# A recurrent attention kernel on one core: the ring for streamed weights goes from six places to five, and 17 instead of 18 weight units are streamed

## The chip, the core and the metric

The kernel runs on one core of one Trainium2 chip. The metric is the device time of one execution in microseconds (us). Before the change it is 1967.8 us, the median of three runs from 1961.2 to 1968.58.

The engines that matter here are TensorE (PE; PEld loads its weights), VectorE (DVE), ScalarE (ACT), and SyncE (SP), which issues nearly all transfers from memory. Each engine works through its own instructions in the order of the program and waits for the others at semaphores. Transfers run on 16 DMA engines that all issuers share.

## The reference, cut to what matters

Two branches work on the normalised input, and both are added to `x`. Branch A is attention with a recurrent memory; branch B is a dense layer pair with gelu.

```python
# S = 2048 rows, Dm = 1024, H = 32 heads of 128, M = 8 memory rows, 32 rows in a segment
mem = mem0
for s in range(64):                                  # one segment after the other
    h = concatenate([mem, xs], axis=1)               # 8 + 32 rows
    q = einsum('btd,dhe->bhte', h, Wq)               # 1024 x 4096 each
    k = einsum('btd,dhe->bhte', h, Wk)
    v = einsum('btd,dhe->bhte', h, Wv)
    p = softmax(where(mask, q k^T * scale, -1e9))
    o = einsum('bhte,hed->btd', p v, Wo)             # 4096 x 1024
    mem = o[:, :M, :]                                # the next segment needs it
    outs.append(o[:, M:, :])
# ...
return x + A(xn, mem0) + B(xn)                       # B: gelu(xn w1 + b1) w2 + b2
```

Each segment needs the 8 memory rows that the segment before it puts out, so the 64 segments can't be run side by side, and each of them needs all four weight matrices. Those have 4 x 8 MB in bf16, which is more than the on-chip memory holds beside everything else.

## The kernel before

Branch B runs first (some 420 us). Then come the 64 segments. The attention weights are cut into 64 units of 128 x 2048 bf16 (0.5 MB). A segment uses them in a fixed order: six half passes of 8 units (K and Q for the first half of the heads, K and Q for the second, V first half, V second half), and then 16 units of O. I write K0 to K7 for the units of a half pass, and O0 to O15 for those of O.

```python
NUNIT = 64
STREAMED = 18
LEAD = 6
LATER = 3
STREAM_BUFS = 6

def pass_order():
    order = []
    for w, u in (("K", 0), ("Q", 0), ("K", 1), ("Q", 1), ("V", 0), ("V", 1)):
        for i in range(KT):                          # KT = 8
            order.append((w, i, u))
    for ch in range(2):
        for j in range(4):
            for u in range(2):
                order.append(("O", ch * 4 + j, u))
    return order

ORDER = pass_order()
PLACED = "S....S.." "..S....S" "...S...S" "...S...S" "....S..." ".S.S..S." ".S..S..S" "..S..S.S"
IS_STREAMED = {unit: PLACED[n] == "S" for n, unit in enumerate(ORDER)}
RESIDENT = [unit for unit in ORDER if not IS_STREAMED[unit]]

IN_PSUM = [unit for unit in ORDER if IS_STREAMED[unit]][3]
HALF = [unit for unit in ORDER[48:] if IS_STREAMED[unit]][3]
```

46 units are loaded once and stay on the chip (resident). The 18 marked with S pass in each segment through a ring of six places. Two of the 18 are not read from memory after the first segment: IN_PSUM lies in two banks of PSUM (`kept`), and HALF lies half in a bank and half in a home of its own. VectorE copies them from the banks into a ring place, in pieces of 128 x 1024.

```python
RING = [f"xn{k}" for k in range(4)] + [f"w1_{k}" for k in range(16)]
RES_PLACES = list(low) + ["xt0", "xt1"] + RING[STREAM_BUFS:]   # places for residents
RING = RING[:STREAM_BUFS]
# ...
streams = [unit for _ in range(NSEG) for unit in ORDER if IS_STREAMED[unit]]
late_by = [
    LATER if unit == HALF or (unit == IN_PSUM and n >= STREAMED) else 0 for n, unit in enumerate(streams)
]
starts = deque(sorted(range(len(streams)), key=lambda n: (n + late_by[n], late_by[n])))

def start_stream(slot):
    n = starts.popleft()
    unit, t = streams[n], slab(slot)
    if unit in kept_in:
        for c0, bank in kept_in[unit]:
            nc.vector.tensor_copy(out=t[:, c0:c0 + 1024], in_=bank)        # L228
    elif unit in copies:
        nc.sync.dma_start(out=t[:, :], in_=copies[unit])                   # L230
    # ...

def unit_done(unit):
    if IS_STREAMED[unit]:
        start_stream(slot_of.pop(used - 1))          # the place just read takes the next start
        # ...
```

So the n-th start goes out when the streamed unit of six places earlier has been used. The starts of the two kept units stand three places later in the order than their use does (LATER).

A half pass multiplies the 32 rows of the segment with eight units; at some segments a second set of 32 rows (`hL`, the left rows, the last eight of each of four segments) is multiplied with the same units.

```python
def product(w, i, t, lhs, acc, seq):
    for j in range(4):                               # four column groups of TensorE, 128 x 512 each
        nc.tensor.matmul(o, lhsT=lhs[:, i, :], rhs=m, ..., tile_position=(0, 32 * j))      # L690

def half_pass(w, u, left, at):
    # ...
    for i in range(KT):
        t = unit_tile((w, i, u))
        product(w, i, t, hT, ps, range(KT))
        if left and i not in ahead:
            product(w, i, t, hL, psL, order)
        unit_done((w, i, u))
        for fn in at.get(i, ()):
            fn()                                     # scores, sums, values of the half before
    return ps, psL

for s in range(NSEG):
    g, i4 = divmod(s, GRP)                           # GRP = 4: four kinds of segment
    # left rows: K first half at i4 == 3, K second at 0, Q first at 1, Q second at 2,
    #            V first at 0, V second at 3, and twice the columns in O at i4 == 1
    psK, psKL = half_pass("K", 0, left_k[0], {})
    turn_k(psK, 0)                                   # ACT cast L734, then DVE transpose L748: kT
    psQ, psQL = half_pass("Q", 0, left_q[0], {})
    q_left(0)
    turn_q(psQ)                                      # ACT cast, DVE transpose: q_home (in b_oL)
    psK1, psK1L = half_pass("K", 1, left_k[1], {})
    # ... transposes; scores(0) after Q unit 0, sums(0) after Q unit 7
    psQ1, psQ1L = half_pass("Q", 1, left_q[1], at)
    # ...
    psV, psVL = half_pass("V", 0, left_v[0], {})
    at = {0: [scores(1)], 2: [values(0, 0)], 4: [values(0, 1)], 6: [sums(1)]}   # cut
    psV1, psV1L = half_pass("V", 1, left_v[1], at)
    at = {4: [values(1, 0)], 6: [values(1, 1)]}      # cut
    for n, unit in enumerate(O_UNITS):
        t = unit_tile(unit)
        o_product(unit, t, psX)                      # L870
        unit_done(unit)
        for fn in at.get(n, ()):
            fn()
    # psX -> o_sb (ACT L954); up to LEAD = 6 products of the next segment's left rows are made here
    put_mem(o_sb, nxt["hT"], ...)                    # L262 on TensorE, then DVE L266 into hr
```

Of the kernel before, what the change touches and what calls it, by code (L numbers as in the profile page):

```python
# [17 lines left out]
S = 2048  # L18
# [23 lines left out]


NUNIT = 64
STREAMED = 18
LOW = 3
SCRATCH = 512
SMALL = 3584
LEAD = 6
LATER = 3  # L50
STREAM_BUFS = 6


def pass_order():
# [11 lines that stand above are left out]


ORDER = pass_order()
PLACED = "S....S.." "..S....S" "...S...S" "...S...S" "....S..." ".S.S..S." ".S..S..S" "..S..S.S"
IS_STREAMED = {unit: PLACED[n] == "S" for n, unit in enumerate(ORDER)}  # L70
assert PLACED.count("S") == STREAMED
RESIDENT = [unit for unit in ORDER if not IS_STREAMED[unit]]

IN_PSUM = [unit for unit in ORDER if IS_STREAMED[unit]][3]
HALF = [unit for unit in ORDER[48:] if IS_STREAMED[unit]][3]
assert len(RESIDENT) == NUNIT - STREAMED


@with_exitstack
def kernel(  # L80
# [102 lines left out]
    RING = [f"xn{k}" for k in range(4)] + [f"w1_{k}" for k in range(16)]  # L183
    RES_PLACES = list(low) + ["xt0", "xt1"] + RING[STREAM_BUFS:]
    RING = RING[:STREAM_BUFS]
    for k in range(7):
# [19 lines left out]
    def fetch_resident(*places):  # L206
# [7 lines left out]
    late_by = [  # L214
        LATER if unit == HALF or (unit == IN_PSUM and n >= STREAMED) else 0 for n, unit in enumerate(streams)
    ]
# [828 lines left out]
```

The softmax here doesn't subtract the row's maximum and nothing guards it: scores larger than these inputs give would overflow.

## Time and profile before

| | before |
|---|---|
| median of 3 runs | 1967.8 us |
| span of the profiled execution | 1969.5 us |
| PE busy | 1774.1 us (90%) |
| DVE busy | 886.2 us (45%) |
| ACT busy | 599.5 us (30%) |
| DMA moved | 627.06 MB, mean 318 GB/s over the span |
| share of queue q1 (SyncE's transfers) | 82.3% of 16 engines over the span |

The share of an engine over the whole span mixes two stages. In branch B (to about 420 us) TensorE works without a pause and the DMA moves little: 123 GB/s in the first 330 us, with 40% of the DMA engines' time. In the 64 segments the DMA moves 368 GB/s. The change touches the second stage, so windows of that stage are what to look at.

A wait row of the profile names who waited, at which line, for whom, and then the total us, how many times, and the longest. "Issue" as releaser means that the engine stood while nothing that the profile shows released it. A row of the timeline has its start, its duration, engine, line, operation and tiles, and in brackets the idle time of the engine before it with its releaser. Buffer numbers are left out: `u` is any resident or ring place, `Wc_O` any copy of a streamed O unit in memory, `kept` the PSUM banks.

### The profile page before, as it was taken

To read this page: it belongs to the slowest core of one execution; us is meant where nothing else is said; L and a number is where in the kernel's file an instruction comes from. 1 tells how busy PE (TensorE), PEld (TensorE's weight loads), DVE (VectorE), ACT (ScalarE), POOL (GpSimd) and SP (SyncE) were. 2 spreads that over 40 slices of the span, in tenths; PEclk is the share of its full clock that TensorE was granted. 3 is DMA by queue.
4 is the path that set the end of the run, shared out by engine and by line. 5 is a ranking of instruction groups with operands and counts; after the bars stand their busy time and mean duration, and the time that the engine had idled before them with its cause. 6 is when DMAs were issued, how large, how long until landed. Compare 5 with 4: busy or idle time off the path is not lost.

```text
span 1969.5 us, 77311 instructions
## 1 busy us (share of the span) xinstructions
PE 1774.1 (90%) x34307; PEld 980.5 (50%) x34307; DVE 886.2 (45%) x2280; ACT 599.5 (30%) x1355; POOL 276.2 (14%) x538
## 2 busy tenths in 40 slices
PE   7999999989888989888989889889888889899887
PEld 3444444445545544455555545455446445545544
DVE  6656565414444444344444444344444444444433
ACT  6343434312223323222222222223222222222222
POOL 0000000002421112121112111111111111111111
PEclk9999999999999999999999999999999999999999
DMA  9821212789999999999999999999999999999998
GB/s 331 252 55 43 55 43 54 283 308 341 381 381 375 388 366 365 354 356 364 378 358 385 370 363 367 363 358 379 359 356 353 380 338 370 383 369 366 367 369 308
DMA packets 219883, 627.06 MB, mean 318 GB/s; under 512 B 47211, under 2 KB 65307, under 8 KB 219548
## 3 DMA queue, kind: packets, MB, share of 16 engines
q1 hardware_dynamic: 199132, 601.96, 82.3%
q0 software_dynamic: 16320, 17.52, 2.7%
q8 instruction: 268, 4.39, 0.9%
q10 hardware_dynamic: 4096, 2.64, 0.4%
q14 instruction: 67, 0.55, 0.1%
HBM read 607.77 MB, written 30.47 MB: 324 GB/s over the span
## 4 chain that ended last, share of the span: by engine, by line
PE 69%; DMA 16%; issue 7%; DVE 4%; ACT 2%; POOL 1%; ACTq 0%; DVEq 0%; POOLq 0%; SPq 0%
PE acc L690 29%; PE acc L870 15%; PE ps L483 10%; DMA u<-Wc_O 8%; PE ps L532 7%; DMA out_dram<-res 4%; PE ps L567 2%; DMA u<-Wc_V 2%; PE mixed L844 2%; DMA u<-Wc_Q 1%; POOL out_dram L1007 1%; PE acc L844 1%; DVE b_oL L748 1%; PE mixed L794 1%; DVE d_oL L899 1%
## 5 line engine op out<-in xcount | busy, mean ns | idle before, releaser
L690 PE MATMUL acc<-u,hr 128*32 128x512 bf16 x11520 | 789.6, 382 | 28.0 <-issue 15.3
L690 PEld LDWEIGHTS <-hr 128*32 128x32 bf16 x12288 | 354.6, 97 | 291.1 <-issue 62.1
L690 PE MATMUL acc<-u,hrL 128*32 128x512 bf16 x2880 | 265.2, 393 | 25.6 <-issue 13.8
L870 PE MATMUL acc<-u,d_oL 128*32 128x256 bf16 (+1 forms) x3552 | 192.6, 297 | 25.5 <-DMA u<-Wc_O 13.9
L483 PE MATMUL ps<-u 128*128 128x512 bf16 x896 | 195.9, 382 | 2.6 <-ACT u L367 2.6
L870 PEld LDWEIGHTS <-b_oL 128*32 128x32 bf16 (+1 forms) x3552 | 117.1, 104 | 81.9 <-issue 48.8
L870 PE MATMUL acc<-u,b_oL 128*32 128x256 bf16 (+1 forms) x1554 | 119.5, 305 | 30.8 <-issue 29.1
L532 PE MATMUL ps<-u 128*128 128x512 bf16 x672 | 147.0, 379 | 0.0
L228 DVE COPY u<-kept 128x1024 bf16<-128x1024 bf16 x190 | 125.0, 686 | 42.4 <-PE acc L690 19.7
L483 PEld LDWEIGHTS <-u 128*128 128x128 bf16 x896 | 88.1, 98 | 109.2 <-issue 4.0
L870 PEld LDWEIGHTS <-d_oL 128*32 128x32 bf16 (+1 forms) x3552 | 103.4, 100 | 69.2 <-issue 44.2
L690 PEld LDWEIGHTS <-hrL 128*32 128x32 bf16 x3072 | 92.9, 98 | 89.8 <-issue 47.8
L266 DVE CAST hr<-mixed 128x64 bf16<-128x64 f32 x63 | 14.1, 224 | 259.1 <-PE mixed L262 249.5
L870 PE MATMUL acc<-W_O,b_oL 128*32 128x256 bf16 (+1 forms) x1776 | 115.5, 307 | 12.9 <-issue 12.9
L748 DVE STREAM_TRANSPOSE b_oL<-b_oL 128x512 bf16<-128x512 bf16 x128 | 90.6, 708 | 61.1 <-ACT b_oL L734 61.1
L844 PEld LDWEIGHTS <-v 32*128 32x128 bf16 x2048 | 64.3, 91 | 101.3 <-issue 70.8
L924 POOL DMA_DIRECT2D res<-hr_d x59 | 33.2, 562 | 537.2 <-PE mixed L825 297.4
L734 ACT CAST kT<-acc 128x512 bf16<-128x512 f32 x64 | 37.4, 585 | 220.0 <-PE acc L690 220.0
L532 PEld LDWEIGHTS <-u 128*128 128x128 bf16 x672 | 65.3, 98 | 77.4 <-DVE g_u L499 0.4
L738 ACT CAST v<-acc 128x512 bf16<-128x512 f32 x128 | 75.3, 589 | 78.4 <-PE acc L690 78.4
L734 ACT CAST b_oL<-acc 128x512 bf16<-128x512 f32 x128 | 75.4, 589 | 76.8 <-PE acc L690 76.8
L1007 POOL DMA_DIRECT2D out_dram<-res x124 | 63.5, 516 | 227.5 <-DVE res L969 226.0
(143 smaller groups left out, 2225.7 us busy)
## 6 DMA issues: line engine op xcount, KB each, us to landing
u<-Wc_O SPq DMA_DIRECT2D x320, 512.0 KB
u<-Wc_K SPq DMA_DIRECT2D x256, 512.0 KB
u<-Wc_V SPq DMA_DIRECT2D x256, 512.0 KB
u<-Wc_Q SPq DMA_DIRECT2D x192, 512.0 KB
u<-in_B_w_dram SPq DMA_DIRECT2D x14, 512.0 KB
u<-in_A_Wq_dram SPq DMA_DIRECT2D x13, 512.0 KB
u<-in_A_Wv_dram SPq DMA_DIRECT2D x12, 512.0 KB
u<-in_A_Wk_dram SPq DMA_DIRECT2D x9, 512.0 KB
```

The costliest lines, as they stand in the source:

```text
L228: nc.vector.tensor_copy(out=t[:, c0:c0 + 1024], in_=bank)
L483: nc.tensor.matmul(ps[:, :].rearrange("p (s t) -> p s t", t=SEG), lhsT=w1_sb[fb // 14 * 8 + kt][:, (fb % 14) * P:(fb % 14 + 1) * P], rhs=x ...
L532: nc.tensor.matmul(ps[:, :], lhsT=gts[fc // 4][:, fc % 4, t * P:(t + 1) * P], rhs=w2_sb[fc // 2][:, fc % 2, cs], start=(fc == 0), stop=(fc ...
L567: nc.tensor.matmul(pss[2 * t + nb][:, :], lhsT=gts[fc // 4][:, fc % 4, t * P:(t + 1) * P], rhs=w2_sb[fc // 2][:, fc % 2, nb * 512:nb * 512 ...
L690: nc.tensor.matmul(o, lhsT=lhs[:, i, :], rhs=m, start=(i == seq[0]), stop=(i == seq[-1]), tile_position=(0, 32 * j),)
L734: cp(out=out, in_=ps.rearrange("p (h e) -> p h e", e=32))
L738: cp(out=t[:, :], in_=ps[:, :])
L748: nc.vector.transpose(out=home, in_=home)
L844: nc.tensor.matmul(oV[b][:, c, :], lhsT=V[q, c * P:(c + 1) * P], rhs=prA[q, c, :], start=(c == 0), stop=False, skip_group_check=True, tile ...
L870: nc.tensor.matmul(acc[r:r + n // 8, 0:n], lhsT=lhs[:, 4 * (i % 4) + 2 * u + k, :], rhs=w_k[:, n * jq:n * jq + n], start=(unit == O_UNITS[ ...
L924: eng.dma_start(out=st["res"][:, :], in_=hr_d[s + 1, :, 256:512])
L1007: nc.gpsimd.dma_start(out=out_flat[rows, 256 * j:256 * j + 256], in_=res[32 * j:32 * j + NX, :])
```

## The change: five places, 17 units, and another placement

The ring gets one place less, and the place that it gives up (`w1_1`) becomes the home of one more resident unit. So 47 units are resident, 17 are streamed, and 15 of these come from memory in each segment. At the same time the streamed units are chosen anew. The purpose is to read one unit less from memory in each segment.

```diff
-STREAMED = 18
+STREAMED = 17
 LOW = 3
 SCRATCH = 512
 SMALL = 3584
 LEAD = 6
 LATER = 3
-STREAM_BUFS = 6
+STREAM_BUFS = 5
@@
 ORDER = pass_order()
-PLACED = "S....S.." "..S....S" "...S...S" "...S...S" "....S..." ".S.S..S." ".S..S..S" "..S..S.S"
+PLACED = "S......." "S..S...S" ".......S" "......SS" ".....S.." ".S..S..." ".SS.S..S" "..SS..S."
```

The eight strings are the half passes K, Q, K, Q, V, V and the two halves of O. Counted in units of the order from 0 to 63, the streamed ones stood at 0, 5, 10, 15, 19, 23, 27, 31, 36, 41, 43, 46, 49, 52, 55, 58, 61, 63 and now stand at 0, 8, 11, 15, 23, 30, 31, 37, 41, 44, 49, 50, 52, 55, 58, 59, 62. IN_PSUM is at 15 in both (Q7 of the first half); HALF was at 58 (O10) and is at 55 (O7).

## The prediction, made before the changed kernel was run

> **What bounds the kernel now.** I read the windows view first. The small matmuls that carry the memory to the next segment (L262) stand once at the end of each segment: at 489.23 us after segment 1 and at 1942.08 us after segment 62. Between them lie 61 segments.
>
> ```profile
> core 0: us, PE busy (x) PEld busy (x) DVE busy (x) ACT busy (x) POOL busy (x), PEclk, DMA share, GB/s
> 489.23:1942.08 1452.85, 1287.64 (x30800) 750.50 (x30797) 614.70 (x1596) 412.50 (x1037) 249.86 (x467) 0.98 0.98 368
> ```
>
> The last two columns matter: over 1452.85 us the 16 DMA engines were 98% busy. One segment lasts 1452.85 / 61 = 23.82 us. TensorE is busy 1287.64 / 61 = 21.11 us of it and idle 2.71 us. Next, the DMA issues of the page tell what keeps the DMA busy:
>
> ```profile
> u<-Wc_O SPq DMA_DIRECT2D x320, 512.0 KB
> u<-Wc_K SPq DMA_DIRECT2D x256, 512.0 KB
> u<-Wc_V SPq DMA_DIRECT2D x256, 512.0 KB
> u<-Wc_Q SPq DMA_DIRECT2D x192, 512.0 KB
> ```
>
> Together 1024 transfers, 16 for each of 64 segments. Eighteen units are streamed, but two (IN_PSUM and HALF) are kept on the chip and copied into the ring by VectorE. Third, the waits of TensorE in the same window, for whether the DMA really holds it:
>
> ```profile
> PE acc L870 <- issue: 53.4, 37, 2.8
> PE acc L690 <- issue: 37.5, 34, 2.5
> PE acc L870 <- DMA u<-Wc_O: 15.4, 31, 1.5
> PE acc L690 <- DVE kL L734: 8.6, 15, 0.8
> ```
>
> The columns are total us, times and longest us. "Issue" names no releaser. I read these stops as DMA waits too, because the chain of waits puts rows "DMA u<-Wc_O" of 7 to 8 us (one at 683.98, one at 779.69) before the stops in O. All rows of these two kinds sum to 115.7 + 24.0 = 139.7 us, or 2.29 us a segment. Waits on VectorE and ScalarE sum to 20.1 us, 0.33 a segment. So the recurrent stage is **DMA bound**, with TensorE close behind: without DMA waits it would need 21.11 + 0.33 + about 0.1 of small gaps = 21.5 us.
>
> **What the Trainium skill says.** "DMA: Bandwidth & Descriptors", section "Issuing engines are not separate DMA queues", says that transfers from all issuing engines run on the same 16 DMA engines; so a transfer removed from SyncE's queue frees time for everything. The share of 0.98 over all queues agrees. Its section "Specifications" gives about 358 GB/s from HBM for a core; the window shows 368 moved, reads and writes together, so I use the measured rate. The section "Anatomy of one DMA — SWDGE (gpsimd) path" gives some 2.0 us of fixed cost, mostly completion, and says that the wait for a semaphore is at the issuing sequencer, before dispatch. That is for GpSimd's path; the ring is filled by SyncE, and no run here isolates its fixed cost, so 2 us for it is an estimate of mine from that page. "VectorE: DVE Perf Modes", section "Why PSUM operands drop a tier", says that a PSUM operand holds a copy to the mode of two bf16 a cycle; the copies out of the kept bank take 683 ns for 1024 columns, 1.5 a ns, which fits.
>
> **The change part by part.**
>
> *Removed: one transfer a segment.* 368 GB/s x 23.82 us = 8.77 MB move in a segment; 16 x 0.524 MB = 8.39 MB of it, 95.7%, is the stream. The DMA is busy 0.98 x 23.82 = 23.34 us, so the stream takes 22.33 us and one transfer 1.40 us. With 15 the busy time is 23.34 - 1.40 = **21.94 us**. If nothing else changed, and the DMA stayed 98% busy, a segment would last 22.4 us and the kernel would gain 63 x 1.4 = 90 us. That is the ceiling, not the prediction.
>
> *Added: nothing in arithmetic.* The matmul and VectorE instructions are the same in number. The freed ring place holds one more resident unit, loaded once.
>
> *Moved, first: the copies of IN_PSUM.* IN_PSUM is still Q unit 7 of the first half, the fourth streamed unit. LATER = 3 puts its start behind those of the three following, at place 6 of the order of starts. With six places it begins when streamed unit 0 is done, with five when streamed unit 1 is done. Unit 0 is K0, at the head of the segment; unit 1 was K5 and is now Q0. VectorE works in program order, so the two copies now come behind the transpose of kT; before, they came ahead of it. The timeline of before:
>
> ```profile
> 699.47 1.29 DVE L228 COPY u<-kept 128x1024 bf16<-128x1024 bf16 x2 [0.46 <-PE acc L690]
> 701.25 0.58 ACT L734 CAST kT<-acc 128x512 bf16<-128x512 f32 x1 [3.20 <-PE acc L690]
> 701.87 0.71 DVE L748 STREAM_TRANSPOSE kT<-kT 128x512 bf16<-128x512 bf16 x1 [1.11 <-ACT kT L734]
> 702.97 0.58 ACT L734 CAST b_oL<-acc 128x512 bf16<-128x512 f32 x1 [1.13 <-PE acc L690]
> ```
>
> The columns are start, duration, engine, line, tiles and the idle time before. Two casts 1.72 us apart, for a half pass of 8 units: 0.215 us a unit, TensorE not waiting. Before, the copies are over at 700.76 and Q7 runs at about 702.97 - 0.2 - 0.215 = 702.55. After, they start when the transpose ends, at 702.58, and are over at 703.87; with 0.1 for the semaphore Q7 can start at 703.97, so TensorE stands for about **1.4 us** in three of four segments. In the fourth, where the left rows of Q add two products in this half pass (+0.43), it is 0.95. Mean 1.27 us. This is a new wait on the path of TensorE: 21.5 + 1.27 = **22.8 us** of TensorE a segment, now more than the 21.94 of the DMA.
>
> *Moved, second: HALF.* It is now O unit 7 (was 10), started when O unit 2 is done. Four units and two groups of value products lie between, about 4 x 0.215 + 2 x 0.56 = 2.0 us (0.56: the step between product groups around a value group at 711 us). VectorE first ends the chain of the sums (some 0.6 us after that start, an estimate from the casts and products at 714 us) and then copies for 0.69 us, so 1.3 us. It fits; I charge nothing.
>
> *Moved, third: a shorter and less even ring.* A transfer now starts when the unit five places earlier is done. With transfers landing every 21.94 / 15 = 1.46 us, the DMA keeps busy only if that release comes about 2 us before the landing of the transfer ahead, so TensorE may lag 4 x 1.46 - 2 = 3.9 us behind a landing (5.3 with six places). The new placement is sparse in K and Q and dense in O. I followed one segment by hand from the landing of O unit 14, the last streamed: K0 is done 2.2 us later (O14 and O15, then 1.4 us from the last O product to the first of K, as at 721.6 to 723.04 us), Q0 at 3.9, Q7 at 6.8 with the new stall, K7 of the second half at 8.6, Q6 at 11.0. Q6 landed at 7.3, so the lag is 3.7: just within the limit. The dense O units then let TensorE run into the next landings. Segments differ, however. TensorE busy time, segment by segment between the L262 groups, is about 21.1, 22.8, 19.4 and 21.4 us for the four kinds of segment (i4 = 0 to 3); the second (doubled O products) ends nearly 2 us behind the DMA, and the next one's lag at Q6 is then 5.5, which leaves the DMA idle some 1.5 us. With some tenths in the others I get 2.6 us of DMA idle in four segments, 21.94 + 0.65 = 22.6 us.
>
> **Sum.** TensorE's path gives 22.8 us, the DMA's 22.6. Two limits this close never hide in each other wholly: I add 0.3 us for waits on transfers that remain. 23.1 us against 23.82, times 63 segments: 45 us. The stages before 465 us differ by one fetch each way, and I charge nothing. 1967.8 - 45 = **1922 us**.
>
> **Rivals.** *The DMA stays the bound and the ring is long enough*: 1878 us. For it speaks the 0.98 share and that TensorE waits mostly for transfers; against it the order of the copies on VectorE, which is fixed by the program. *The short ring starves*: TensorE would wait in O for transfers that started late, the DMA share would fall to 0.92 or less (21.94 / 23.82), and the gain would be gone: 1960 to 1985 us. For it speak the eight-unit gaps that are followed by three adjacent pairs; against it that the margin at the tightest point comes out at zero and not negative. *TensorE takes it all*: no wait on transfers is left and only the copies hold it, 22.8 us a segment, 1903 us.
>
> **Range and chances.** Half of the stall or half of the DMA idle time being wrong moves a segment by 0.4 us, 25 us in all. 1893 to 1952 us should hold it 8 times in 10. Faster by over 2% means below 1928 us, hardly above my figure: 0.57. Within 2%: 0.38. Slower by over 2% needs the starving ring at its worst: 0.05.
>
> **What would show it.** Right: the issues count 960 transfers; a row "PE acc L690 <- DVE u L228" of some 60 to 80 us among TensorE's waits, absent now; the copies in the timeline behind the kT transpose; DMA share near 0.95 over the same segments. Wrong: a share still at 0.98 with 22.4 us a segment (first rival), or a share near 0.92 with waits on Wc_O transfers of 2 us a segment and more (second). What would make it wrong most easily is the stall falling where TensorE would wait for a transfer anyway.

## The result, and the profile after

The changed kernel takes 2030.98 us (median of 4 runs, 2027.09 to 2040.29). Against the kernel before, the ratio is 1.0343, with a 95% interval from 1.0298 to 1.0388: it is **slower by 3.4%**. The prediction was 1922 us with a range to 1952, so it missed in size and in direction.

The same views as before, now of the changed kernel. First the windows view over the same 61 segments (the memory products of L262 end segment 1 at 490.26 us and segment 62 at 1996.30 us):

```profile
core 0: us, PE busy (x) PEld busy (x) DVE busy (x) ACT busy (x) POOL busy (x), PEclk, DMA share, GB/s
490.26:1996.30 1506.04, 1297.94 (x30800) 725.85 (x30797) 610.80 (x1596) 412.45 (x1037) 249.89 (x467) 0.98 0.94 333
```

A segment takes 1506.04 / 61 = 24.69 us instead of 23.82. The DMA share fell only from 0.98 to 0.94, while the rate fell from 368 to 333 GB/s. So the DMA engines were busy for 0.94 x 24.69 = 23.2 us a segment, nearly as long as before (23.3), for one transfer less.

The transfers are as many as counted, 960, 15 a segment (from the page's DMA issues):

```profile
u<-Wc_O SPq DMA_DIRECT2D x384, 512.0 KB
u<-Wc_Q SPq DMA_DIRECT2D x256, 512.0 KB
u<-Wc_V SPq DMA_DIRECT2D x192, 512.0 KB
u<-Wc_K SPq DMA_DIRECT2D x128, 512.0 KB
```

TensorE's waits in the window (total us, times, longest):

```profile
PE acc L870 <- DMA u<-Wc_O: 99.3, 147, 2.5
PE acc L690 <- DVE u L228: 49.5, 56, 1.2
PE acc L870 <- issue: 21.8, 21, 2.6
PE acc L690 <- DMA u<-Wc_Q: 8.7, 15, 1.3
PE acc L690 <- DVE kL L734: 5.1, 15, 0.8
```

Two things stand here. The second row is new: TensorE waits for the copies of the kept unit, 49.5 us. And the waits on transfers are not gone although a transfer is: all rows with a transfer or "issue" as releaser sum to 110.7 + 27.1 = 137.8 us, against 139.7 before. They now gather in O (the rows at L870). The new wait came on top instead of taking the place of an old one.

Three of the four signs that the prediction had named for being right are there: 960 transfers, the copies behind the transpose, and a DMA share near 0.95. The fourth, the wait for the copies, is there with 49.5 us instead of 60 to 80. None of the four bears on the term that turned out wrong, the waits on transfers.

The timeline of VectorE shows the order that the prediction described: the transpose of kT first, then the two copies.

```profile
1016.41 0.71 DVE L748 STREAM_TRANSPOSE kT<-kT 128x512 bf16<-128x512 bf16 x1 [2.65 <-ACT kT L734]
1017.05 1.25 DVE L228 COPY u<-kept 128x1024 bf16<-128x1024 bf16 x2
```

And TensorE, in the same stretch, stands at Q7 until they end at 1017.05 + 1.25 = 1018.30:

```profile
1016.75 1.05 PE L690 MATMUL acc<-u,hr 128*32 128x512 bf16 x16 [0.19 <-DMA u<-Wc_Q]
1018.35 1.91 PE L690 MATMUL acc<-u,hr 128*32 128x512 bf16 x32 [0.56 <-DVE u L228]
```

### The profile page after: what moved, and what is told of

Same layout as the page of the kernel before. It is cut to its first block, busy times and chain, and to the rows that moved or that the text cites. A ratio compares the mean times of both kernels' runs of the same rounds, so it can differ in the third digit from the quotient of the medians.

```text
span 2026.5 us, 77236 instructions
## 1 busy us (share of the span) xinstructions
PE 1784.3 (88%) x34307; PEld 954.7 (47%) x34307; DVE 882.1 (44%) x2280; ACT 599.6 (30%) x1355; POOL 276.3 (14%) x538
## 3 DMA queue, kind: packets, MB, share of 16 engines
q10 hardware_dynamic: 4096, 2.64, 0.4%
## 4 chain that ended last, share of the span: by engine, by line
PE 59%; DMA 25%; DVE 8%; issue 4%; ACT 3%; POOL 0%; ACTq 0%; POOLq 0%; SPq 0%; DVEq 0%
PE acc L690 28%; DMA u<-Wc_O 20%; PE ps L483 10%; PE acc L870 8%; PE ps L532 7%; DVE u L228 3%; PE ps L567 2%; DMA u<-Wc_Q 2%; DMA u<-Wc_K 1%; ACT kT L734 1%; PE mixed L844 1%; DVE d_oL L899 1%; DMA out_dram<-res 1%; DVE kL L734 1%; DVE b_oL L748 1%
## 5 line engine op out<-in xcount | busy, mean ns | idle before, releaser
L690 PE MATMUL acc<-u,hr 128*32 128x512 bf16 x11520 | 788.1, 381 | 66.0 <-DVE u L228 50.4
L690 PEld LDWEIGHTS <-hr 128*32 128x32 bf16 x12288 | 337.0, 96 | 340.8 <-issue 98.0
L690 PE MATMUL acc<-u,hrL 128*32 128x512 bf16 x2880 | 254.1, 386 | 8.2 <-DVE kL L734 5.1
L870 PE MATMUL acc<-u,d_oL 128*32 128x256 bf16 (+1 forms) x3330 | 195.4, 298 | 72.3 <-DMA u<-Wc_O 57.5
L870 PEld LDWEIGHTS <-b_oL 128*32 128x32 bf16 (+1 forms) x3552 | 118.9, 105 | 108.7 <-issue 74.9
L870 PE MATMUL acc<-u,b_oL 128*32 128x256 bf16 (+1 forms) x1776 | 120.3, 312 | 50.2 <-DMA u<-Wc_O 46.8
L870 PEld LDWEIGHTS <-d_oL 128*32 128x32 bf16 (+1 forms) x3552 | 102.0, 99 | 127.2 <-issue 105.0
L228 DVE COPY u<-kept 128x1024 bf16<-128x1024 bf16 x190 | 122.9, 672 | 47.4 <-PE acc L870 45.3
L870 PE MATMUL acc<-W_O,b_oL 128*32 128x256 bf16 (+1 forms) x1776 | 113.8, 308 | 5.5 <-issue 5.4
L748 DVE STREAM_TRANSPOSE kT<-kT 128x512 bf16<-128x512 bf16 x64 | 45.5, 711 | 161.4 <-ACT kT L734 161.4
L690 PEld LDWEIGHTS <-hrL 128*32 128x32 bf16 x3072 | 83.6, 97 | 63.5 <-issue 21.2
L954 ACT CAST d_oL<-acc 128x256 bf16<-128x256 f32 (+1 forms) x63 | 26.9, 427 | 234.7 <-PE acc L870 234.7
```

Source lines behind the costliest of these rows:

```text
L690: nc.tensor.matmul(o, lhsT=lhs[:, i, :], rhs=m, start=(i == seq[0]), stop=(i == seq[-1]), tile_position=(0, 32 * j),)
L748: nc.vector.transpose(out=home, in_=home)
L870: nc.tensor.matmul(acc[r:r + n // 8, 0:n], lhsT=lhs[:, 4 * (i % 4) + 2 * u + k, :], rhs=w_k[:, n * jq:n * jq + n], start=(unit == O_UNITS[ ...
L954: nc.scalar.copy(out=o_sb[:, 0:no, :], in_=psX[:, 0:32 * no].rearrange("p (h e) -> p h e", e=32))
```

## The experiments

Four explanations were put against each other. "Places": a ring place makes a round trip (release, issue, queue, landing, use), and fewer places deliver less. "Copy stall": the copies behind the transpose. "Placement": the units bunched in O. "Bandwidth": the reading of my prediction, that a DMA 98% busy is at its limit and five places keep it there.

### The ring alone: 18 units and five places

```diff
 # the kernel before
-STREAM_BUFS = 6
+STREAM_BUFS = 5
```

> The kernel before with nothing changed but the ring, five places instead of six (18 streamed units, 16 transfers a segment, the placement of before; the freed place takes a resident, and one late home is left empty). Theory 'places' (a place makes a round trip from its release over issue, queue, landing and use, and the number of places sets how many transfers are under way): in the changed kernel one transfer with five places comes out every 1.64 us (24.6 us / 15), so 16 of them need 26.3 us a segment, 2.5 us more than before, and the time is about 2100 to 2130 us. Theory 'copy stall' (VectorE's copies behind the transpose of kT hold TensorE): the copies stay ahead of the transpose here, so about 1965 to 1975 us. Theory 'placement' (the clustering in O is what costs): 1965 to 1985 us. Theory 'bandwidth' of my prediction (98% busy is saturation, five places suffice): 1965 to 1985 us.

Measured: 2009.36 us (4 runs), ratio 1.0193, interval 1.0126 to 1.026. One place less costs about 1.9%, some 38 us (44 us between the medians; a ratio here is not that of two medians, and the two ways differ by up to 7 us). The same 61 segments, again between L262 groups:

```profile
487.59:1977.85 1490.26, 1302.00 (x30800) 739.65 (x30796) 609.78 (x1596) 412.76 (x1037) 250.83 (x467) 0.99 0.97 358
```

They take 37 us more than before, and TensorE's waits on transfers sum to 171.9 us instead of 139.7. That refutes "bandwidth" and says that neither the copies nor the placement are needed for a loss; but it is less than half of what "places" in its simple form expected, so none of the four ranges holds it.

### The changed kernel with six places

```diff
 # the changed kernel
-STREAM_BUFS = 5
+STREAM_BUFS = 6
@@ def fetch_late(unit):
+            if unit == RESIDENT[-1]:
+                res_tiles[unit] = res_tiles[RESIDENT[-2]]
+                return
```

The sixth place and the 47 residents together need 4 KB more in each partition than there is. Here one resident O unit has no home, and another one's weights stand in for it, so the output is not the reference's while every matmul stays.

> The changed kernel with six places instead of five and its own placement of 17. The memory for the sixth place is found by leaving one resident O unit without a home (the last O unit is multiplied with the weights of another resident one; all instructions stay, the output is not the reference's). Theory 'places': 15 transfers at the 1.49 us of before are 22.3 us a segment, 95 us less than before, and with TensorE's path near it about 1880 to 1920 us. Theory 'copy stall': the copies start one use earlier, so only the 50 us of waits on the copies go: about 1975 us. Theory 'placement': 1990 to 2020 us.

Measured: 1938.04 us (4 runs), ratio 0.9826 (0.9769 to 0.9884). With the sixth place the same placement is 93 us faster than the changed kernel. This edit also moves the start of the copies one use earlier, so it holds both effects. The time lies in none of the three ranges: better than "copy stall" and "placement" allow, and short of "places". The next experiment has the copies early with five places, at 1985.33 us; so some 47 us are left for the sixth place.

### The copies ahead of the transpose again

```diff
-PLACED = "S......." "S..S...S" ...
+PLACED = "S......S" "...S...S" ...
```

> The changed kernel with one streamed unit moved by one unit, from Q0 to K7 of the first half, so that VectorE's copies of the kept Q unit stand ahead of the transpose of kT again; five places, 17 streamed. Theory 'copy stall': the 50 us of TensorE's waits on the copies go, and the time is about 1975 to 1985 us. Theory 'places': the transfers set the pace and TensorE waits for them elsewhere instead; 2010 to 2030 us. Theory 'placement': 2020 to 2030 us.

Measured: 1985.33 us (20 runs), ratio 1.0096 (1.0075 to 1.0117), 46 us less than the changed kernel. The row "DVE u L228" is gone from TensorE's waits, which now begin:

```profile
PE acc L870 <- DMA u<-Wc_O: 95.3, 128, 2.9
PE acc L870 <- issue: 17.6, 17, 2.0
PE acc L690 <- issue: 9.5, 12, 2.8
```

Waits on transfers sum to 142.7 us here, against 137.8 in the changed kernel: almost nothing of the 49.5 us moved there. The stall was a cost of its own, and "copy stall" gave the number (the upper end of its range). It does not explain why the kernel is still slower than before.

### An even spread with five places

```diff
-PLACED = "S......." "S..S...S" ".......S" "......SS" ".....S.." ".S..S..." ".SS.S..S" "..SS..S."
+PLACED = "S....S.." "..S....S" "....S..." ".S....S." "....S..." ".S.S..S." ".S..S..S" "..S..S.S"
```

> Five places and 17 streamed units with the spread of the kernel before (one streamed unit of K and Q dropped, the others moved a little: 0, 5, 10, 15, 20, 25, 30, 36, 41, 43, 46, 49, 52, 55, 58, 61, 63); the copies stand ahead of the transpose as well. Theory 'placement': the loss goes, about 1930 to 1965 us. Theory 'places': an even spread helps somewhat, the round trip stays; 1980 to 2020 us. Theory 'copy stall': about 1975 to 1985 us, as for the run with the unit moved by one.

Measured: 1955.03 us (18 runs), ratio 0.9941 (0.9918 to 0.9965).

```profile
487.96:1918.89 1430.93, 1280.01 (x30800) 742.50 (x30797) 607.42 (x1596) 413.60 (x1037) 250.83 (x467) 0.99 0.96 351
```

A segment takes 1430.93 / 61 = 23.46 us, and the waits on transfers sum to 124.2 us. The spread is worth another 30 us, as "placement" expected in direction and in size. This version does everything that the reference asks and is faster than both kernels, though only by 0.6% against the one before.

### The even spread with six places

The same edit as for the changed kernel with six places, on the even spread; again one resident O unit has no home.

> 17 streamed units spread as before, and six places (one resident O unit without a home, as in the other run with six places; the output is not the reference's). With five places this spread takes 1955 us. If a place is worth what it was worth in the kernel before (2009 against 1966, some 43 us), about 1910 us. If six places make the spread matter little, about 1938 us, as with the clustered placement and six places. If the DMA had been at its limit with five places already, 1955 us.

Measured: 1919.69 us (4 runs), ratio 0.9788 (0.976 to 0.9817), 35 us below five places (30 us by the ratios). A place is worth somewhat less here than with 18 units, and with six places the even spread is still 18 us better than the bunched one. The time lies near the predicted 1922 us, but that is chance: here the ring has six places and the copies stand ahead of the transpose, and the prediction had neither. In its window:

```profile
485.76:1889.53 1403.77, 1266.36 (x30801) 733.63 (x30798) 613.32 (x1596) 412.96 (x1037) 249.88 (x467) 0.99 0.97 358
```

A segment takes 23.01 us, and the waits on transfers still sum to 111.1 us, 1.82 us a segment.

### Without transfers: what TensorE needs alone

```diff
 # on either kernel, from segment 1 on; unchanged lines around these are cut
+        if unit in copies and n >= STREAMED:
+            stream_tiles[n], slot_of[n] = None, slot
+            return
@@ unit_tile
+                if t is None:
+                    return res_tiles[[r for r in RESIDENT if r[0] == unit[0]][0]]
```

The streamed units are multiplied from a resident unit's place; the output is not the reference's.

> The kernel before without its streamed transfers: from segment 1 on, each of the 16 units that come from memory is multiplied from a resident unit's place instead, with the same instructions on TensorE and VectorE; the copies of the two kept units stay. The output is not the reference's. It measures what the segments take when no transfer is waited for. By the idle times of the profile (23.82 us less 2.29 of waits on transfers a segment) 21.5 us a segment, 1966 less 63 x 2.3, about 1820 us. If the waits called issue were something else than transfers, about 1900 us.

> The changed kernel without its streamed transfers, as in the run for the kernel before. Theory 'copy stall': the copies of the kept Q unit are still behind the transpose of kT, and without other waits the stall shows whole, 1.27 us a segment: 63 x 1.27, 80 us more than the kernel before without transfers, about 1900 us. If the copies only seemed to hold TensorE because transfers were late, both kernels take the same without transfers.

Measured: 1745.78 us for the kernel before and 1820.73 for the changed one (2 runs each). The windows views, before first:

```profile
486.29:1719.02 1232.73, 1214.88 (x30800) 699.67 (x30796) 603.73 (x1596) 411.25 (x1037) 249.73 (x467) 1.00 0.07 18
```

```profile
484.42:1790.85 1306.43, 1227.86 (x30800) 708.67 (x30797) 603.72 (x1596) 411.30 (x1037) 249.77 (x467) 1.00 0.07 17
```

That is 20.21 and 21.42 us a segment. The difference, 1.21 us, is the copy stall bare, against 1.27 in the prediction. Of these 1.21 us, 1.00 stands as a wait in the changed kernel (this edit shifts the lines: the copies are at L232, the products at L697):

```profile
PE acc L697 <- DVE u L232: 61.3, 61, 1.2
```

The other 0.21 us are in the busy time, which is 12.98 us longer for 61 more stops. Two other readings of the prediction are settled as well. The "issue" rows of TensorE in these segments disappear when there are no transfers, so they were waits on transfers. But the 20.21 us are 1.3 us below the 21.5 that I had worked out from busy and idle time: TensorE's busy time itself falls from 1287.64 to 1214.88 us, 73 us. Transfers cost TensorE more than its wait rows show. An estimate of mine from these traces gives 62 of the 73 us: the rows of waits on transfers in the kernel before count 147 stops, at 0.21 us each 31 us; and 61 of its 1452.85 us were at half the clock, none without transfers, which makes another 31 us.

### With little TensorE work: what the ring delivers alone

```diff
 # products of units that are not streamed are left out, except the first and last of each sum;
 # the lines that hand u to the product are cut
+                if i not in (seq[0], seq[-1]) and not IS_STREAMED[w, i, u]:
+                    return
@@ o_product
+                if unit not in (O_UNITS[0], O_UNITS[-1]) and not IS_STREAMED[unit]:
+                    return
```

The outputs are not the reference's; transfers, copies and ring stay.

> The kernel before with TensorE's products of units that are not streamed left out (the first and last of each half pass and of O stay; the output is not the reference's). Transfers, copies, ring and placement stay. TensorE then has little more than half its work, and the ring shows how fast it can deliver. If 16 transfers at the full rate are the limit (1.30 us each by the shortest packet time of 159 ns, eight packets an engine, and some 1 us of other traffic in a segment), 22 us a segment, about 1850 us. If a place's round trip is the limit, the 23.4 us of before stay, about 1940 to 1965 us. If the wait chain of the small steps takes over, less than either.

> The same with five places. Theory 'round trip': the transfer time itself grows with fewer places, and five places give 5/6 of the rate of six: if six take 23 us a segment, five take 27, some 250 us more in all. Theory 'buffer' (a place is only worth something because TensorE and the DMA are both near their limits and do not run evenly; with TensorE idle five places deliver as fast as six): within 15 us of the run with six places.

> 17 streamed with the even spread, five places, the same products left out. Against the run with 18 and five places one transfer of 16 is gone: theory 'buffer': 63 x 1.35, 85 us less. Theory 'round trip': the same share of a longer round, 95 to 105 us less.

Measured: 1848.38 us (2 runs), 1961.3 us (18 runs) and 1872.8 us (2 runs). The windows views: 18 units with six places, 18 with five, and 17 (even spread) with five.

```profile
482.54:1815.38 1332.84, 925.60 (x18461) 426.20 (x18461) 614.06 (x1596) 414.00 (x1037) 249.91 (x467) 0.79 1.02 400
```

```profile
480.65:1936.24 1455.59, 989.67 (x18460) 450.78 (x18461) 611.20 (x1596) 414.14 (x1037) 249.85 (x467) 0.72 0.98 366
```

```profile
482.38:1843.43 1361.05, 948.22 (x18705) 442.84 (x18705) 605.79 (x1596) 413.27 (x1037) 249.89 (x467) 0.77 0.99 368
```

Per segment these are 21.85, 23.86 and 22.31 us. With TensorE busy for 68 to 70% of the time, five places deliver 366 to 368 GB/s and six deliver 400: 113 us for one place between the medians. That refutes "buffer", which expected at most 15 us, and it is less than half of the 250 us that "round trip" expected from 5/6 of the rate. With six places the time is the one expected from 16 transfers at the full rate, 22 us a segment and about 1850 us. One unit less at five places saves 88 us, next to the 85 of "buffer" and below the 95 to 105 of "round trip"; this pair does not separate the two well, and its spread differs too.

Count the turns of a place: with 18 uses and six places each place serves 3 units a segment, so a turn takes 21.85 / 3 = 7.28 us; with 18 and five, 23.86 / 3.6 = 6.63; with 17 and five, 22.31 / 3.4 = 6.56. If the turn set the pace at five places, six would allow 3 x 6.6 = 19.8 us; the run takes 21.85, so another limit must hold there, perhaps the rate of 400 GB/s. No run has seven places to show it. That the two runs with five places agree on 6.6 us is no proof of a fixed turn: they agree as well on 1.49 us a transfer (23.86 / 16 and 22.31 / 15). What is shown is that the sixth place raises the rate; the **round trip** as its cause is a reading. The traces fit it: from the issue of a transfer to its last packet, 3.9 transfers were under way on average with six places and 3.3 with five, and a packet of 4096 bytes took 165 and 174 ns on average. In the full kernels it was 3.4 under way before and 3.0 in the changed one, with 173 and 183 ns.

The granted clock was 0.72 to 0.79 in these runs, so the remaining matmuls were slower than usual, and TensorE was busy 64 us longer with 18 units and five places than with six. Part of the 2.0 us between these two runs may come from that. The run with the ring alone has no such difference (0.98 and 0.99), and there a place cost 0.6 us a segment.

### Two other ways to set the units

Both edits are against the changed kernel; its line PLACED is left out. The 15 transfers at equal steps of TensorE's time (scores, values and the handoff counted in):

```diff
+PLACED = "S.....S." "....S..S" "..S....." "S...S..." ".S.....S" "..S..S.." "S...S.S." ".S.S...S"
```

> Five places, 17 streamed, and the 15 that come from memory set at equal steps of TensorE time instead of equal steps of units (0, 6, 12, 18, 24, 28, 33, 39, 42, 45, 48, 52, 54, 59, 63, with the kept ones at 15 and 57), the handoff between segments and the scores and values counted in. If what is left of the loss is unevenness in time: 1925 to 1945 us, better than 1955. If the round trip of a place sets the pace whatever the spread: 1950 to 1965 us. The copies of the kept Q unit start after unit 6 and are ahead of the transpose.

Measured: 1957.24 us (8 runs), ratio 0.9958 (0.994 to 0.9977), the same as the even spread in units (0.9941), and in the range for a limit that does not depend on the fine spread. Between these two spreads it does not matter.

And the kept units later in the order:

```diff
-LATER = 3
+LATER = 4
+PLACED = "S...S..S" ".......S" "....S..." ".S....S." "....S..." ".S.S..S." ".S.S.S.." "..S..S.S"
```

> Five places, 17 streamed, and the two kept units start four places later in the order instead of three, so that each takes its ring place for a shorter time (between the start of the copy and the use); the streamed units before each kept one are moved a little ahead so that the copies still fit (0, 4, 7, 15 and 49, 51, 53, 58; the others as in the even spread). If a place's round trip sets the pace, a kept unit that holds a place for one use less gives the others more places: 1935 to 1950 us, better than 1955. If the holding does not count: 1950 to 1960 us. If the copies come too late and hold TensorE again: 1965 us and more, with waits on the copies among TensorE's waits.

Measured: 1986.19 us (4 runs), ratio 1.0105 (1.0063 to 1.0146), 31 us worse than the even spread. That is in the range for late copies, but no wait on the copies is among TensorE's waits, so none of the three expectations holds. Over the stretch from 490 to 1961.6 us its waits on transfers sum to 144 us, against 124 in the window of the even spread. The run changed two things at once (LATER, and four units moved), so whether a kept unit's hold on its place counts stays open; the units from memory stand less evenly too (none between 7 and 20).

## Why the prediction was wrong, step by step

The prediction's own sum, in us a segment, beside what the window of the changed kernel shows:

| | predicted | measured |
|---|---|---|
| TensorE busy | 21.11 | 21.28 |
| waits on VectorE and ScalarE, small gaps | 0.43 | 0.34 |
| wait for the copies | 1.27 | 0.81 |
| waits on transfers | 0.3 | 2.26 |
| a segment | 23.1 | 24.69 |

- **The step that failed: "I add 0.3 us for waits on transfers that remain".** They were 137.8 / 61 = 2.26 us, nearly the 2.29 of before; all other terms together came out 0.4 us too high. The prediction had laid a DMA path of 22.6 us beside a TensorE path of 22.8 and let the longer one hide the other. The paths did not overlap like that in any run that has both. In the even spread a segment took 23.46 us, 1.15 above its ring with little TensorE work (22.31), and the waits on transfers were 2.04 us; even with six places and the even spread they were 1.82.
- **The bound.** "So the recurrent stage is DMA bound" rested on the share of 0.98, and the DMA path was built on it. The share was right, but not its reading: with six places and little TensorE work the same 16 transfers ran at 400 GB/s and 21.85 us a segment. The kernel before, at 23.82, sat 2.0 us above that and 3.6 us above TensorE without transfers (20.21). Neither limit alone gives its time.
- **"One transfer 1.40 us".** The busy time of the DMA was taken as work that shrinks with the transfers. It was to be 21.94 us and was 23.2. Of 333 GB/s x 24.69 us = 8.22 MB, the stream is 7.86 MB, 95.7%, so a transfer took 23.2 x 0.957 / 15 = 1.48 us of busy time. The same working gives 1.42 us for 18 units with five places and for the even spread with six, and 1.34 with six places and little TensorE work: the busy time of a transfer is no fixed cost. Whether its growth is a cause of the loss or follows from it, the runs do not say.
- **The copies.** Right in mechanism and order, and nearly in size where the stall stands alone (1.21 us against 1.27; the prediction's own three times 1.4 and once 0.95 have a mean of 1.29). In the changed kernel 49.5 / 61 = 0.81 us a segment of it shows, and moving one unit by one takes 46 us away. The prediction feared most that the stall would fall where TensorE waits for a transfer anyway. A part of it did: the bare stall costs 75 us in all (1745.78 to 1820.73), in the full kernel 46.
- **HALF.** Nothing was charged. The waits name only L690 for the copies, and HALF is used at L870, so this holds.
- **The shorter ring and the placement.** I saw that five places leave a lag of 3.9 us and that O is dense, but charged 0.65 us a segment for both, with a landing every 1.46 us whatever the number of places. By the ratios the runs put one place at 38 us with the placement of before (18 units) and 30 us with the even spread (17 units), and the bunched placement at another 30 us.
- **The rivals.** "The short ring starves" came nearest: TensorE did wait in O for transfers. But it left the copies out, and its 1960 to 1985 us are too low by 46 us or more. Its signs did not quite come: the share was 0.94 instead of 0.92, and the waits named Wc_O were 99.3 / 61 = 1.63 us a segment instead of 2.

The runs split the loss into steps, each the difference of two ratios and known to some 0.3 to 0.7%, in shares of the time before (1966 us): one place less, +1.9% (38 us); one unit less, in an even spread, -2.5% (50 us); the bunched spread, +1.5% (30 us); the copies behind the transpose, +2.5% (49 us). Together they give the measured +3.4%, as they must, since each step starts where the one before it ends; in another order the shares could differ. The first two steps are the exchange that the change was made for, and it is worth 0.6%. The placement that came with it costs 4.0%, copies included.

What stays open: what a place's turn consists of and whether it is what limits five places, how fast the bunched placement would be with little TensorE work, and the run with LATER = 4.

## What to carry to other kernels

A busy share near 1 on the DMA engines does not say that they are at their limit: compare the rate with a run in which the consumer has little work before you count on time per transfer staying fixed. A ring's depth is part of its rate, so a place given up for less traffic has to be weighed against it, best by a run with one place less and nothing else changed; here that cost 1.9%, and the unit saved brought 2.5%. And when units are placed anew, follow what else is triggered by the same event: here a shift of one unit put two copies behind a transpose and cost about as much (49 us) as the saved transfer brought (50 us).

## What the runs showed of the hardware that I had not expected

- The DMA share of the profile stays near 1 while the rate differs by 9%: 1.02 at 400 GB/s (18 units, six places, little TensorE work), 0.98 at 366 (the same with five), 0.98 at 368 (the kernel before). In the trace of the kernel before, the packets of 4096 bytes between 500 and 1900 us take 159 ns in the median (156 at least) and 173 ns in the mean; in the changed kernel the median is the same and the mean 183. The mean of a transfer depends on how many were still under way when it was issued (kernel before, counted from issue to last packet): 200 ns behind one, 180 behind two, 167 behind three, 163 behind four. So in this trace a packet's time, which counts as busy, is longer on average when fewer transfers are under way.
- A single core moved 400 GB/s, reads and writes together. The Trainium skill, "DMA: Bandwidth & Descriptors", section "Specifications", gives about 358 GB/s from HBM for a core, as half of what one stack gives to two cores; this program ran on a single core, and the stream of weights alone came at 16 x 0.524 MB in 21.85 us, 384 GB/s.
- TensorE's busy time for the same 61 segments was 1287.64 us with the transfers and 1214.88 without, at a granted clock of 0.98 and 1.00. The clock explains about 2% of the 6%; about as much again are the stops, by the estimate above.
